# Issuing two of four output stores behind the attention transposes, in a fused attention and MLP kernel

## The chip, the cores and the metric

The kernel runs on one core of a Trainium2 chip. The metric is the device time of one execution in microseconds (us); less is better. Where several executions were timed, the median is given.

## The reference

The first half is sliding-window causal attention for 8 batches, 8 heads, 576 positions and head dimension 64; a query sees itself and the 63 keys before it. The second half is an MLP with a hard-swish over all 4608 rows.

```python
# q, k, v: [8, 8, 576, 64]
scores = (q @ k.T) / sqrt(64)
mask = (rel >= 0) & (rel < 64)            # rel = query position - key position
attn = softmax(where(mask, scores, -1e9)) # over keys
x = (attn @ v).transpose(0, 2, 1, 3).reshape(4608, 512)
h = x @ w_in                              # w_in: [512, 2048]
g = h * clip(h + 3, 0, 6) / 6
out = g @ w_out                           # w_out: [2048, 512], out is float32
```

Matmuls are done in bf16 with sums in f32; inputs and output are f32.

## The kernel before, in words

**Two loops that interleave.** The rows of the MLP are cut into 9 blocks T of 512 tokens. For each block, `s1(T)` (L787) makes h and g: 8 chunks of two 128-wide slices of d_ff, 64 or 128 matmuls (L812), each chunk in one of three PSUM pairs of banks; ACT makes a relu of it (L821), DVE the product (L824) into gT, which frees the pair. Then `s2(T)` (L832) multiplies g with w_out: four output tiles ts = 0 to 3 of 128 rows, 16 matmuls each (L860), so 64 steps n. When a tile is done, `finish` (L870) has ACT copy it from PSUM to an SBUF tile osb (L878), and SP store that tile to the output (256 KB, L883). There are three osb tiles, so the copy of a tile waits for the store of the third tile before it: the copy of ts = 3 waits for the store of ts = 0 of the same block.

**Attention runs inside s2.** During s2(T) TensorE also does the attention of batch b = T + 1, in units put at fixed steps n (`REST`, L925): scores at n = 11 and 18 (L672), products with V at n = 25 (two) and n = 35 (two) (L699). For each of the four groups g of two heads, DVE normalises the product (L737, L740) into a tile opg, and for batches 2 to 7 SP transposes that tile by DMA into xT (L747, in `xdma`); these are called x0 to x3 here. s1(T + 1) reads xT; its first chunk takes the matmuls that need x3 last (L805).

**What else is on the queues.** SP also issues the two DMA transposes of q and k of the batch after that (QKT, L437) once s1(T + 1) is planned to begin, and after these the loads of q (L458, L479) and k (L479) for the batch after that; their f32 data are cast on POOL before they are transposed. ACT issues the loads of v (L384) between its own work.

**Who sets the order.** The order of each engine's queue is written out by a planner, `Plan` (L37), when the kernel is built. Every operation is put into a heap with the time at which it is expected to be ready, a duration, and keys of other operations that must have been placed (`deps`); it is popped in the order of these times, and only then the instruction is emitted. A DMA's duration comes from `moved` (L269). `pl.mark` (L55) notes that a key is done and at what time. An operation whose key isn't marked is parked until it is. So `deps` set the place in a queue; the semaphores that engines wait for on the chip come from the data. In the table of keys, ("x", b, g) is the landing of an x transpose, ("st", nst) that of a store with nst = 4T + ts, ("op", b, g) the normalisation.

The stores of tiles 0 and 1 become ready at about n = 16 and n = 32 of s2, and those of tiles 2 and 3 at n = 48 and 64.

Of the kernel before, what the change touches and what calls it, by code (L numbers as in the profile page):

```python
# [105 lines left out]
def kernel(  # L106
# [11 lines left out]
    B, H, S, D = q.shape  # L118
    DM, FF = moe_w_in.shape
    NT = B * S  # L120
    NG = H // 2
# [3 lines left out]
    SP = KB * P  # L125
# [10 lines left out]
    NR6 = 2  # L136
# [3 lines left out]
    pl = Plan()  # L140
# [21 lines left out]
    def two_banks(readers, dt=F32):  # L162
        i = min(range(len(psums)), key=free_at)
        while free_at(i) >= 1e9:
            pl.pop()
            i = min(range(len(psums)), key=free_at)
        for r in held[i]:
            pl.wait(r)
        held[i] = readers
        return psums[i].tile([P, 2, 512 if dt == F32 else 1024], dt, name=f"ps{i}", tag="ps")  # L170
# [98 lines left out]
    def moved(now, kb, rate):  # L269

        dma["t"] = max(dma["t"], now) + kb / rate
        land = dma["t"] + 1.9 + dma["lag"]
        return max(now + 0.06, dma["t"] - 5.0), land
# [293 lines left out]
    def soft(b, g):  # L567
        return [("mask", b, g)] if b else [("exp", b, g, i) for i in range(2)]

    def vcasts(b, g):  # L570
        return [("cast", b, 2, g // 2, kb) for kb in range(KB)] if b == 0 else [("cast", b, 2, kb) for kb in range(KB)]
# [120 lines left out]
    def pv64(b, g, o):  # L692

        V, W, pT = V_ring[b % 2], W_ring[b % 2], halves.pop((b, g))
        for h in range(2):
            for m in range(KB):
                for odd in range(2):
                    i = min(2 * m + odd, BL - 1)
                    nc.tensor.matmul(  # L699
                        o[odd * D : (odd + 1) * D, h, m * VW : (m + 1) * VW],  # L700
                        lhsT=pT[:, h, i * D : (i + 1) * D],
                        rhs=(V if i % 2 else W)[:, g, m, h, :], start=True, stop=True,
                    )
        pl.pe(0.5)

    def pv128(b, g, o):
        V = V_ring[b % 2]
        pT = P_ring[(b * NG + g) % NPT]
        for h in range(2):
            for qb in range(KB):  # L710
                ob = o[:, h, qb * VW : (qb + 1) * VW]
                nc.tensor.matmul(
                    ob, lhsT=pT[:, h, qb, 0:P], rhs=V[:, g, qb, h, :],
                    start=True, stop=(qb == 0),
                )
                if qb:
                    nc.tensor.matmul(
                        ob, lhsT=pT[:, h, qb - 1, P : 2 * P], rhs=V[:, g, qb - 1, h, :],
                        start=False, stop=True,
                    )  # L720
        pl.pe(0.55)

    def pv(b, g):
        for r in soft(b, g) + vcasts(b, g):
            pl.wait(r)
        o = two_banks([("op", b, g)])
        if b >= NR6:
            pl.need(("w0", b % 2))
            pv64(b, g, o)
        else:  # L730
            pv128(b, g, o)
        pl.mark(("pv", b, g), pl.t)
        ov = o[:, :, 0 : KB * VW].rearrange("p h (k w) -> p h k w", w=VW)
        cell = {}
        def norm(s):
            rec = small.tile([P, 2, KB], F32, name="rec", tag="rec")
            nc.vector.reciprocal(out=rec[:].unsqueeze(3), in_=ov[:, :, :, D:VW])  # L737
            opg = opool.tile([P, KB, 2, D], BF16, name="opg", tag="opg")
            cell["o"] = opg
            nc.vector.tensor_tensor(  # L740
                out=opg[:].rearrange("p k h d -> p h k d"), in0=ov[:, :, :, 0:D],
                in1=rec[:].unsqueeze(3).to_broadcast([P, 2, KB, D]), op=MULT,
            )
        def xdma(t):
            def fn(s):
                x0 = x_at(b)
                nc.sync.dma_start_transpose(  # L747
                    out=xT[:, g, x0 : x0 + SP].rearrange("d (k t) -> d k t", t=P),
                    in_=cell["o"][:].rearrange("p k h d -> p (k h d)"),
                )  # L750
                fr, land = moved(s, 164, 230)
                pl.free["SP"] = fr
                return land
            pl.op("SP", t, 0.1, fn, ("x", b, g))
        m = b * NG + g - 4
        first = (("mask", b, NG - 1),) if b >= NR6 and g == 1 else ()
        pl.op("DVE", pl.t + 0.1, 1.05, norm, ("op", b, g), None if b < NXP else xdma,
              deps=first + ((("x", m // NG, m % NG),) if m >= 0 else ()))
        return cell
# [110 lines left out]
    def finish(T, ts, acc, c0, c1):  # L870
        rows = out[T * TB : (T + 1) * TB]
        rows = rows.rearrange("(p j) d -> j p d", j=J)[ts] if T >= NR6 else rows[ts * P : (ts + 1) * P]
        nst = T * 4 + ts + (c0 > 0)
        cell = {}
        def cp(s):
            osb = osbp.tile([P, DM], F32, name="osb", tag="osb")
            cell["o"] = osb
            nc.scalar.copy(out=osb[:, c0:c1], in_=acc[:, c0:c1])  # L878
            if c0:
                nc.scalar.dma_start(out=rows[:, c0:c1], in_=osb[:, c0:c1])  # L880
        def store(t):
            def fn(s):
                nc.sync.dma_start(out=rows[:, c0:c1], in_=cell["o"][:, c0:c1])  # L883
                fr, land = moved(s, 262, 375)
                pl.free["SP"] = fr
                return land
            pl.op("SP", t, 0.1, fn, ("st", nst))
        pl.op("ACT", pl.t + 0.1, 0.62, cp, ("acc", nst), None if c0 else store,
              deps=(("st", nst - 3),) if nst >= 3 else ())

# [35 lines left out]
    for T in range(NTB):  # L926
# [3 lines left out]
        b = T + 1  # L930
# [36 lines left out]
```

The softmax here doesn't subtract the row's maximum and nothing guards it: scores larger than these inputs give would overflow.

## Time and profile before

| what | value |
|---|---|
| median of 4 runs | 307.53 us (306.58 to 308.46) |
| profiled execution, its time | 308.46 us |
| its span, from first to last instruction | 306.7 us |
| granted TensorE clock, mean | 0.999 |
| busy: TensorE, VectorE, ScalarE, GpSimd | 97%, 54%, 50%, 39% |
| s2's matmuls (L860), busy | 132.7 us |
| s1's matmuls (L812), busy | 126.5 us |
| stores on SP (L883) | 36, median 3.8 us from issue to landing |
| x transposes on SP (L747) | 24, median 3.7 us to landing |
| QKT transposes on SP (L437) | 12, median 8.4 us to landing |

The engines are called PE (TensorE; PEld is its weight load), DVE (VectorE), ACT (ScalarE), POOL (GpSimd) and SP (SyncE, which only issues DMAs). In rows of groups the numbers after the first bar are busy time in us and the mean ns of one instruction, those after the second bar are the idle time of the engine just ahead of the group and what ended most of it. In a timeline a row starts with start and length in us; a number in square brackets is the engine's idle time ahead of it. For a DMA on SPq or ACTq the length is that of the issue, not of the transfer; its landing is the time at which its semaphore says that the data have arrived. In the chain of work, a DMA's piece is the time from issue to landing. In rows of windows, after the limits, come length, then busy us (and number) of PE, PEld, DVE, ACT and POOL, the granted clock, the busy share of the DMA engines and GB/s.

### The profile page before, as it was taken

The numbers are of one execution on the slowest core, as the hardware profiler recorded it, in microseconds if no ns is written. First come the engines' busy times: TensorE is split into PE (matmuls) and PEld (weight loads), VectorE is DVE, ScalarE is ACT, GpSimd is POOL, SyncE is SP. The second block draws the span as 40 slices with busy tenths as digits, with TensorE's granted clock in tenths as the row PEclk, the third lists the DMA queues.
The fourth block names the chain that finished last, engine by engine and source line by source line (L and its number), as shares of the span: only waits on it lengthen the run. The fifth ranks groups of instructions, "written<-read, shape, count | busy, mean of one in ns | idle before, by whom it ended". The sixth has DMA issues, their size and how long they took to land.

```text
span 306.7 us, 6681 instructions
## 1 busy us (share of the span) xinstructions
PE 296.7 (97%) x2787; PEld 153.1 (50%) x2787; DVE 164.1 (54%) x209; ACT 154.8 (50%) x190; POOL 118.9 (39%) x185
## 2 busy tenths in 40 slices
PE   7989989998999999999989999999999999999995
PEld 2554445643544454875434454445665544444443
DVE  5585678656734664466526562667275617304610
ACT  5856686455616661566146713672367236316611
POOL 3167547618834482477027722682252000000000
PEclk9999999999999999999999999999999999999999
DMA  7999999999999999999699979997990550010011
GB/s 218 258 371 387 389 315 252 255 161 286 232 189 238 278 178 156 235 280 190 137 193 280 236 117 225 259 231 121 244 198 11 124 92 0 34 71 34 0 69 71
DMA packets 134863, 58.38 MB, mean 190 GB/s; under 512 B 117296, under 2 KB 124720, under 8 KB 134832
## 3 DMA queue, kind: packets, MB, share of 16 engines
q1 hardware_dynamic: 106560, 50.80, 73.2%
q10 hardware_dynamic: 28272, 7.15, 12.4%
q8 instruction: 22, 0.36, 0.6%
q14 instruction: 9, 0.07, 0.1%
HBM read 36.70 MB, written 9.44 MB: 150 GB/s over the span
## 4 chain that ended last, share of the span: by engine, by line
PE 71%; DMA 14%; SPq 6%; POOL 2%; ACT 2%; issue 2%; DVE 1%; ACTq 0%; POOLq 0%
PE acc L860 33%; PE ps L812 32%; DMA st<-in_moe_w_out_dram 5%; DMA QKT<-nat 3%; DMA st<-in_v_dram 3%; PE ps L699 2%; SPq L357 2%; PE ps L672 2%; DMA xT<-opg 2%; SPq L332 2%; SPq L415 1%; ACT pT L678 1%; POOL wout L280 1%; POOL V L280 1%; DMA tl<-in_k_dram 0%
## 5 line engine op out<-in xcount | busy, mean ns | idle before, releaser
L824 DVE SCALAR_TENSOR_TENSOR gT<-t,ps 128x1024 bf16<-128x1024 bf16 x72 | 87.7, 1220 | 97.3 <-ACT t L821 97.3
L860 PE MATMUL acc<-wout,gT 128*128 128x512 bf16 (+2 forms) x592 | 132.7, 374 | 0.8 <-DVE wout L277 0.5
L812 PE MATMUL ps<-xT,win 128*128 128x512 bf16 (+4 forms) x704 | 126.5, 340 | 2.2 <-DMA xT<-opg 1.3
L821 ACT ACTIVATE t<-ps,half 128x1024 bf16<-128x1024 f32 x72 | 79.9, 1113 | 51.4 <-PE ps L812 50.0
L812 PEld LDWEIGHTS <-win 128*128 128x128 bf16 x704 | 65.2, 98 | 62.1 <-issue 2.9
L860 PEld LDWEIGHTS <-gT 128*128 128x128 bf16 x592 | 54.6, 98 | 61.5 <-issue 1.4
L878 ACT COPY osb<-acc 128x512 f32<-128x512 f32 (+2 forms) x37 | 21.4, 578 | 75.8 <-PE acc L860 72.9
L280 POOL CAST runs<-st 64x512 bf16<-64x512 f32 (+1 forms) x49 | 30.3, 619 | 71.0 <-DMA st<-in_v_dram 55.4
L280 POOL CAST nat<-st 128x512 bf16<-128x512 f32 x48 | 35.2, 758 | 9.8 <-DMA st<-in_k_dram 7.1
L678 ACT ACTIVATE pT<-ps 128x768 bf16<-128x768 f32 x36 | 26.9, 837 | 9.3 <-PE ps L672 9.3
L683 DVE TENSOR_TENSOR pT<-pT,mask 128x1152 bf16<-128x1152 bf16 x24 | 22.2, 944 | 14.9 <-ACT pT L678 14.9
L740 DVE TENSOR_TENSOR opg<-ps,rec 128x640 bf16<-128x640 f32 x32 | 26.4, 824 | 1.1
L280 POOL CAST V<-st 128x512 bf16<-128x512 f32 (+1 forms) x30 | 19.0, 636 | 4.4 <-DMA st<-in_v_dram 2.7
L622 ACT ACTIVATE pT<-ps 128x768 bf16<-128x768 f32 x16 | 12.7, 833 | 0.9 <-PE ps L613 0.8
L277 DVE CAST runs<-st 128x576 bf16<-128x576 f32 x14 | 7.9, 568 | 6.9 <-DMA st<-in_q_dram 5.1
L279 ACT COPY QKT<-ps 128x1152 bf16<-128x1152 bf16 x8 | 9.1, 1135 | 4.2 <-PE ps L582 4.2
L699 PEld LDWEIGHTS <-pT 128*64 128x64 bf16 x480 | 8.6, 111 | 5.1 <-issue 3.0
L280 POOL CAST wout<-st 128x1024 bf16<-128x1024 f32 x6 | 7.4, 1251 | 7.9 <-DMA st<-in_moe_w_out_dram 7.9
L699 PE MATMUL ps<-runs,pT 128*64 128x65 bf16 x288 | 9.9, 196 | 0.0
L672 PEld LDWEIGHTS <-QKT 64*128 64x128 bf16 x432 | 7.3, 95 | 5.1 <-issue 5.1
L699 PE MATMUL ps<-V,pT 128*64 128x65 bf16 x192 | 9.5, 197 | 0.0
L672 PE MATMUL ps<-QKT 64*128 64x64 bf16 x432 | 9.1, 194 | 0.0
(60 smaller groups left out, 119.9 us busy)
## 6 DMA issues: line engine op xcount, KB each, us to landing
out_dram<-osb SPq DMA_DIRECT2D x35, 256.0 KB, 4.1
st<-in_q_dram SPq DMA_DIRECT2D x12, 512.0 KB, 6.8
st<-in_k_dram SPq DMA_DIRECT2D x24, 256.0 KB, 6.3
st<-in_v_dram ACTq DMA_DIRECT2D x24, 256.0 KB, 5.8
st<-in_moe_w_out_dram SPq DMA_DIRECT2D x4, 1024.0 KB, 13.3
st<-in_moe_w_in_dram SPq DMA_DIRECT2D x3, 1024.0 KB, 10.4
st<-in_q_dram SPq DMA_DIRECT2D x8, 288.0 KB, 6.7
st<-in_k_dram SPq DMA_DIRECT2D x8, 288.0 KB, 7.1
```

Source lines behind the costliest of these rows:

```text
L280: return lambda s: nc.gpsimd.tensor_copy(out=out_ap, in_=in_ap) and None
L622: nc.scalar.activation(out=pT[:, :, kbs[0] : kbs[0] + 2, 0:QW], in_=st[:, :, 0 : 2 * QW].rearrange("p h (k w) -> p h k w", k=2), func=EXP, ...
L672: nc.tensor.matmul(st[:, h, c * D : (c + 1) * D], lhsT=kwin(b, g, i, h), rhs=turned(qk(b, 0, g), i)[h * D : (h + 1) * D], start=True, stop ...
L678: nc.scalar.activation(out=pT[:, :, part * NB * D : (part + 1) * NB * D], in_=st[:, :, 0 : NB * D], func=EXP, scale=scale,)
L683: pl.op("DVE", t, 0.8, lambda s: nc.vector.tensor_tensor(out=P_half, in0=P_half, in1=mask64[:].unsqueeze(1).unsqueeze(1).to_broadcast([P, ...
L699: nc.tensor.matmul(o[odd * D : (odd + 1) * D, h, m * VW : (m + 1) * VW], lhsT=pT[:, h, i * D : (i + 1) * D], rhs=(V if i % 2 else W)[:, g, ...
L740: nc.vector.tensor_tensor(out=opg[:].rearrange("p k h d -> p h k d"), in0=ov[:, :, :, 0:D], in1=rec[:].unsqueeze(3).to_broadcast([P, 2, KB ...
L812: nc.tensor.matmul(hs, lhsT=win16[:, g, (2 * c + j) * P : (2 * c + j + 1) * P], rhs=xs, start=(g == 0), stop=(g == NG - 1),)
L821: nc.scalar.activation(out=t1[:], in_=hT[:], func=RELU, bias=half[:], scale=1.0 / 6.0)
L824: nc.vector.scalar_tensor_tensor(out=gT[:, 2 * c : 2 * c + 2, :], in0=cell["t"][:], scalar=1.0, in1=hT[:], op0=MIN, op1=MULT,)
L860: nc.tensor.matmul(accs[ts][:, c0:c1], lhsT=gT[:, fc, ts * P : (ts + 1) * P], rhs=wout16[:, fc, c0:c1], start=(fc == 0), stop=(fc == NFC - 1),
L878: nc.scalar.copy(out=osb[:, c0:c1], in_=acc[:, c0:c1])
```

## The change

The x transposes mark a new key ("xi", b, g) with the time of their issue. In s2(T) with T from 1 to 6, that is beside the attention of batches 2 to 7, the stores of tiles 0 and 1 get the key of x3 as a dependence, so that the planner places them on SP's queue after x3. Before, their places followed from the times at which their copies were done.

```diff
@@ xdma, in pv @@
                     in_=cell["o"][:].rearrange("p k h d -> p (k h d)"),
                 )
+                pl.mark(("xi", b, g), s)
                 fr, land = moved(s, 164, 230)
                 pl.free["SP"] = fr
                 return land
@@ store, in finish @@
                 fr, land = moved(s, 262, 375)
                 pl.free["SP"] = fr
                 return land
-            pl.op("SP", t, 0.1, fn, ("st", nst))
+            held_back = NR6 <= T + 1 < B and ts < 2
+            pl.op("SP", t, 0.1, fn, ("st", nst), deps=(("xi", T + 1, NG - 1),) if held_back else ())
```

NR6 is 2, B is 8 and NG is 4.

## Prediction

> **What bounds the kernel now.** I read the page's busy times first, then its costliest groups, then the stages as windows, the chain of work that ended last, and the timelines of SP, ACT and DVE around the change. The busy times, and the one group of TensorE that waits for anything near the change:
>
> ```profile
> PE 296.7 (97%) x2787; PEld 153.1 (50%) x2787; DVE 164.1 (54%) x209; ACT 154.8 (50%) x190; POOL 118.9 (39%) x185
> L812 PE MATMUL ps<-xT,win 128*128 128x512 bf16 (+4 forms) x704 | 126.5, 340 | 2.2 <-DMA xT<-opg 1.3
> ```
>
> TensorE works for 97% of the span. The column after the second bar is its idle time ahead of the first matmul (s1): 2.2 us in all, 1.3 of them for an x transpose. The row of s2's matmuls (L860) shows 0.8, those of the attention (L672, L699) 0.0. So the change cannot win more than these 2.2 us, and probably only the 1.3.
>
> Where they are is seen in windows from the start of one s1 to that of the next (a window's length follows its limits):
>
> ```profile
> 122.66:153.76 31.10, 31.10 (x345) 20.12 (x344) 17.94 (x20) 15.47 (x18) 15.03 (x23) 1.00 1.00 211
> 153.76:186.32 32.56, 31.28 (x282) 14.93 (x281) 16.55 (x20) 15.48 (x18) 15.00 (x23) 1.00 1.12 207
> 186.32:217.26 30.94, 30.94 (x281) 14.86 (x280) 17.92 (x20) 15.47 (x18) 14.76 (x23) 1.00 1.13 208
> ```
>
> Only the middle one is longer than its PE work, by 32.56 - 31.28 = 1.28 us. The chain names the cause:
>
> ```profile
> 149.91 0.91 SPq L747
> 150.82 0.05 issue
> 150.91 5.55 DMA xT<-opg
> 156.46 0.04 issue
> 156.51 12.68 PE ps L812 x58
> ```
>
> The last x transpose of batch 4, issued at 150.91, lands at 156.46. s1(4) began at 153.76, did the 6 matmuls that don't need it (1.46 us), and stood from 155.22.
>
> SP's queue in s2(2) and in s2(3), where L883 is the store and L747 the x transpose:
>
> ```profile
> 111.11 0.36 SPq L883 DMA_DIRECT2D out_dram<-osb  x1
> 114.57 1.24 SPq L747 DMA_TRANSPOSE xT<-opg  x1
> 115.90 0.53 SPq L883 DMA_DIRECT2D out_dram<-osb  x1
> 116.52 4.66 SPq L747 DMA_TRANSPOSE xT<-opg  x3
> 121.28 0.53 SPq L883 DMA_DIRECT2D out_dram<-osb  x1
> ...
> 142.55 0.57 SPq L883 DMA_DIRECT2D out_dram<-osb  x1
> 146.30 1.24 SPq L747 DMA_TRANSPOSE xT<-opg  x1
> 147.63 0.53 SPq L883 DMA_DIRECT2D out_dram<-osb  x1
> 148.26 3.88 SPq L747 DMA_TRANSPOSE xT<-opg  x3
> 152.23 0.53 SPq L883 DMA_DIRECT2D out_dram<-osb  x1
> ```
>
> Store 0 goes out some 3.5 us ahead of the first x transpose, store 1 between the first and the second, store 2 right behind the fourth.
>
> **Part one: what leaves the path of the x transposes.** Store 0 was issued and had landed (4.1 to 4.6 us) by about the time at which x0 was issued, and x0 waits for its normalisation (DVE ends it at 114.53, the issue is at 114.57). So store 0 is worth nothing here. Store 1 costs its issue, 0.53 us and a gap. But x1 needs its own normalisation: that ends at 116.19 in s2(2) and 147.93 in s2(3), so x1 can move up from 116.52 and 148.26 only by some 0.3 us (0.5 in s2(1)). After that three issues of 1.24 us with gaps of 0.08 run on SP, and the normalisations are ahead of them. Besides, in s2(2), s2(4) and s2(5) one of the three issues took 1.98, 1.71 and 1.71 us in place of 1.24, and x1 landed 4.4, 4.3 and 5.1 us after its issue; in the other three stages 2.9, 2.6 and 2.7. In those same stages store 1 landed late (4.3 to 4.5 us, against 2.8 in s2(3) and s2(6)). I read this as a queue filled by store 1, so x3 wins another 0.5 to 0.7 us there: about 0.3 us earlier in s2(3) and s2(6), 0.5 in s2(1), 0.8 to 1.0 in the others.
>
> What is that worth? x3 lands at +1.1, +0.7, +2.7, +0.5, +1.1 and 0.0 us from the start of the s1 that reads it (s2(1) to s2(6)), and is needed at about +1.4. Only the third is late. An issue 0.3 us earlier takes 0.3 of its 1.28 us for sure; the rest depends on the landing, which took 5.5 us there and 3.4 to 4.8 in the other five. Store 1 was no part of that, for it had landed at 150.4, before x3 was issued. With a landing of the others' kind, x3 comes at 150.6 + 3.9 = 154.5, and all 1.28 us are gone. I take that: the 5.5 is the one outlier. The ends are a gain of 0.3 and of 1.28; a loss here is possible only if the stores now close behind x3 slow it, and store 2 stood there before.
>
> **Part two: what is put behind x3.** Two stores of 0.53 us and gaps, 1.2 us of SP, stand ahead of store 2 and the two QKT transposes. With x3 earlier by 0.3 to 1.0, these are issued 0.2 to 0.9 us later, and with 512 KB more in the queue ahead of them. At store 2's 3.5 to 4.7 us to landing I allow 2 us more in all. QKT has cover: in s2(3) the second one is issued at 157.56 and lands 8.6 us later, at 166.2; the scores that read it begin at 171.56. That is 5.4 us, and 4.9 to 5.5 around the other stages. The k loads that wait for QKT end at 142.45 in s2(3), 3.8 us ahead of x0 (146.30), and at 173.7 in s2(4), 4.1 us ahead. The casts on POOL for the next QKT end at 146.3 in s2(3), against an issue at 152.87. All this costs nothing while the delay stays below 3.8 us; every microsecond beyond would be one of x0, and then of x3.
>
> **Part three: the new wait.** There are three output tiles (osb), so the fourth copy of a stage (ACT, L878) waits until store 0 has landed. That was long so; now store 0 is issued just behind x3. In ACT's queue the relus of the next s1 stand behind that copy, behind them the DVE products and the PSUM banks that TensorE's fourth chunk needs. From ACT and DVE around the start of s1(3), at 122.66:
>
> ```profile
> 122.91 0.58 ACT L878 COPY osb<-acc 128x512 f32<-128x512 f32 x1 [2.91 <-PE acc L860]
> 124.61 1.11 ACT L821 ACTIVATE t<-ps,half 128x1024 bf16<-128x1024 f32 x1 [1.12 <-PE ps L812]
> 125.75 1.22 DVE L824 SCALAR_TENSOR_TENSOR gT<-t,ps 128x1024 bf16<-128x1024 bf16 x1 [7.51 <-ACT t L821]
> ```
>
> The copy can begin as late as 124.0 without moving the relu (ACT has 1.12 us of idle time there). DVE frees the first bank pair at 125.75 + 1.22 = 126.97, and TensorE comes to its fourth chunk at 122.66 + 3 x 13.97/8 = 127.90: another 0.93 us. So the wait is hidden while store 0 lands before s1's start + 2.3 us. Beyond that each microsecond is one of TensorE, in each of six stages.
>
> Nearest row for store 0: store 2 of today, issued at the same place right behind x3. It lands 3.8, 3.5, 4.7, 3.7, 3.8 and 3.7 us after its issue in s2(1) to s2(6). Store 0's issue, by the times of part one, is at about 88.9, 120.2, 151.95, 183.4, 215.1 and 245.35. That makes landings at +0.9, +1.0, +2.9, +0.8, +1.7 and +0.7 from the next s1. Five are hidden; the one in s2(3) costs 0.6 us if the bad landing recurs, nothing with the others' 3.8. The ends: with the 5.5 us of the slowest x transpose everywhere, the overrun is 0.3 + 0.75 + 1.4 + 0.3 + 1.0 + 0.2 = 3.95 us; with the slowest of all stores (7.3 us) 1.8 us more per stage, 14.8 in all. Less than nothing is excluded, since the wait is new.
>
> Against the change speaks a rule of the Trainium skill (DMA: Bandwidth & Descriptors, on HWDGE ordering): a DMA's completion increment is written only after every earlier write of the same DMA engine, on whatever queue. By it store 0 waits also for the first v load, which ACT issues 0.4 to 1.3 us ahead of x3's end and which lands at 92.7, 122.8, 154.0, 186.3 and 218.1, that is +0.9, +0.1, +0.2, 0.0 and +0.8: before my landings. The second v load starts with the very copy that waits (122.93), so it can't precede store 0. Rule and row give the same sum; I keep the row, because store 2 has already paid for all of this.
>
> **The sum.** The profiled execution took 308.46 us, 306.7 of it span and 1.76 around it. Less 1.28, plus 0 to 0.6, that is 307.2 to 307.8. The median of the four runs, 307.53, is 0.93 below this execution, so a typical run seems to lose less to such a late landing than the one shown: the gain from the median is perhaps 0.4, and I forecast 307.1. The fastest run, 306.58, is roughly what a run without the wait takes.
>
> **Rivals.**
> (a) Nothing happens: x3's landing is set by what lies around it, store 0 is hidden. 307.5. For it: 5.5 us had nothing to do with store 1.
> (b) The fourth copy becomes the bound. Three stores, then QKT, next to v loads that take 5.3 to 7.4 us to land at this place: store 0 lands 5.5 us after issue, beyond the +2.3 at which it decides, 3.95 us are added and the 1.28 won: 307.53 + 2.7 to 3.95 = 310.2 to 311.5, taken as 310.6. Against it: store 2's own landings.
> (c) More is won than one wait: x3 up to 1 us earlier spares other runs all their late landings, 307.53 - 2.2 = 305.3 at most; taken as 305.8.
> (d) The order doesn't come out as meant, since a planner writes the queues: its copy may take another place on ACT. By the planner's costs store 0 lands at about 17.1 us of s2 and the copy is due at 17.55, so I expect ACT's order as it is; otherwise the copy falls behind the first relu, which costs nothing: 307.5.
>
> **Chances.** Forecast 0.43 (306.3 to 308.0 as its own range), (a) and (d) together 0.25, (b) 0.27, (c) 0.05. A measurement here can tell 0.5%, 1.54 us, from no change: below 305.99 is faster, 0.05; above 309.07 slower, 0.25, since a small overrun of (b) stays within; within 0.70. The range reaches from 306.1 to 310.4: it leaves out (c) and the upper half of (b).
>
> **What would show it.** Right: SP shows four x transposes in a row, the last three within 3.9 us, then three stores; the wait of L812 for xT falls from 1.3 to below 0.3; the fourth copy starts up to 1.3 us later in a stage while the relu behind it moves by less than 0.6. Wrong: L878 waits for out_dram, and L812 for the DVE product (gT) in several stages, or L672 waits for QKT.

## The result and the profile after

The changed kernel takes 308.6 us (median of 43 runs) against 307.7 us for the kernel before (64 runs in the same comparison): ratio 1.0028, 95% interval 1.0014 to 1.0042. That is about 0.9 us more, inside the stated range, but the other way than the forecast of 307.1 us. The same kernel was measured twice more beside the experiments, with 1.0065 (1.0040 to 1.0091) and 1.0038 (1.0014 to 1.0062).

The execution that was profiled with the result was disturbed (1716.76 us, the matmuls of s1 and s2 over four times their length), so the lines below are from the run "after_second" of the same kernel: 307.7 us, of which 306.0 are span. Its code is one to two lines longer, so L813 is the L812 of before, L861 is L860, L822 is L821, L879 is L878 and L884 is L883.

The busy times and the groups that answer to those shown of before, with ACT's relu and copy added (after the second bar: idle time ahead of the group, and what ended it):

```profile
PE 297.1 (97%) x2787; PEld 153.1 (50%) x2787; DVE 163.4 (53%) x209; ACT 154.0 (50%) x190; POOL 120.1 (39%) x185
L813 PE MATMUL ps<-xT,win 128*128 128x512 bf16 (+4 forms) x704 | 127.0, 340 | 1.0 <-DVE gT L825 0.7 <-DMA xT<-opg 0.3
L822 ACT ACTIVATE t<-ps,half 128x1024 bf16<-128x1024 f32 x72 | 79.5, 1114 | 41.1 <-PE ps L813 34.9 <-POOL runs L280 3.2 <-DVE gT L825 2.9
L879 ACT COPY osb<-acc 128x512 f32<-128x512 f32 (+2 forms) x37 | 21.4, 579 | 86.1 <-PE acc L861 58.2 <-DMA out_dram<-osb 23.3 <-PE ps L813 4.6
```

ACT's same two groups in before:

```profile
L821 ACT ACTIVATE t<-ps,half 128x1024 bf16<-128x1024 f32 x72 | 79.9, 1113 | 51.4 <-PE ps L812 50.0 <-DVE gT L824 1.3
L878 ACT COPY osb<-acc 128x512 f32<-128x512 f32 (+2 forms) x37 | 21.4, 578 | 75.8 <-PE acc L860 72.9 <-DMA st<-in_v_dram 2.9
```

TensorE's idle time for x is shorter (0.3 us instead of 1.3), as meant. In its place it now waits for gT, the product that frees a PSUM pair, and ahead of that ACT stands: its copies wait 23.3 us for stores (about 2.9 us ahead of each of these copies it stood idle before too, for TensorE), and its relus show 3.2 us "for POOL", of which nothing was seen before. SP around s2(4) and s1(5):

```profile
175.83 7.00 SPq L747 DMA_TRANSPOSE xT<-opg  x4
182.92 1.49 SPq L884 DMA_DIRECT2D out_dram<-osb  x3
184.51 9.34 SPq L437 DMA_TRANSPOSE QKT<-nat  x2
193.94 0.53 SPq L884 DMA_DIRECT2D out_dram<-osb  x1
```

Four x transposes in a row, then three stores, then QKT: the order is what the change says. No other queue's order changed.

The five s1 that follow a changed s2 and have attention around them are compared best by their own length, from the first L813 to the first L861. Undisturbed they take 13.81 us (13.97 where x comes in two pieces, s1(3) and s1(6)). Three of them, s1(2), s1(4) and s1(5), of after_second:

```profile
90.53:104.67 14.14, 13.97 (x65) 6.25 (x64) 7.71 (x7) 8.31 (x8) 7.01 (x12) 1.00 1.19 271
...
153.06:166.89 13.83, 13.83 (x66) 6.24 (x65) 7.62 (x7) 8.19 (x8) 5.98 (x10) 1.00 1.27 224
184.02:198.82 14.80, 14.12 (x65) 6.25 (x64) 7.79 (x7) 8.07 (x8) 7.00 (x12) 1.00 1.21 244
```

The excess of the five is 0.33 + 0.17 + 0.02 + 0.99 + 0.39 = 1.90 us. In the trace of before it was 1.54, 1.45 of it in s1(4), for the one late x transpose. The place of the loss has changed: s1(4) is clean, s1(5) lost a microsecond.

What each piece waited for is seen when the starts of the matmuls are laid beside those of an undisturbed s1 of the same kind in before: where the distance grows by a step, TensorE lost time, and the matmul there has a releaser. The largest step of after_second, in s1(5):

```profile
197.10 1.89 PE L813 MATMUL ps<-xT,win 128*128 128x512 bf16 x8 [0.68 <-DVE gT L825]
```

This is the eighth and last chunk, and the step is 0.84 us. (It is more than the idle time shown, because the ends of matmuls are modelled.) Of the 1.90 us, 0.81 are steps for xT (s1(2) 0.33, s1(5) 0.16, s1(6) 0.32), so the x transposes are not always in time now either. Steps for gT at the eighth chunk make 1.01 (s1(3) 0.17, s1(5) 0.84), and one at the fourth chunk, in s1(6), 0.07. In after_again, the other trace of the changed kernel, the excess is 1.21: 1.16 for gT at the eighth chunk (0.28, 0.22 and 0.66 in s1(2), s1(3) and s1(5)), 0.05 at the fourth, none for x.

The traces with the old order (before, before_osb4, before_oneq, before_osb4_oneq, before_tailsp below) have 1.54, 0.50, 0.50, 0.26 and 1.87 us, and those with one store held 0.30 and 1.63, all of it for x. These sums scatter too much, from one execution to the next, to stand for the 0.9 us that was measured. But TensorE waits for gT in these five s1 only where both stores are held.

### The profile page after: what moved, and what is told of

It reads as the page before. It is cut to its first block, busy times and chain, and to the rows that moved or that the text cites. A ratio compares the mean times of both kernels' runs of the same rounds, so it can differ in the third digit from the quotient of the medians.

```text
span 1715.0 us, 6681 instructions
## 1 busy us (share of the span) xinstructions
PE 1710.8 (100%) x2787; PEld 541.8 (32%) x2787; DVE 159.0 (9%) x209; ACT 160.5 (9%) x190; POOL 107.9 (6%) x185
## 4 chain that ended last, share of the span: by engine, by line
PE 100%; DVE 0%; ACT 0%; issue 0%; ACTq 0%
PE acc L861 45%; PE ps L813 44%; PE ps L699 2%; PE ps L672 2%; PE ps L582 1%; PE ps L613 1%; PE ps L607 1%; PE ps L898 1%; PE ps L712 1%; PE ps L766 1%; PE ps L717 1%; DVE idle L204 0%; ACT osb L879 0%; ACTq L879 0%
## 5 line engine op out<-in xcount | busy, mean ns | idle before, releaser
L861 PE MATMUL acc<-wout,gT 128*128 128x512 bf16 (+2 forms) x592 | 770.7, 1658 | 0.0
L813 PE MATMUL ps<-xT,win 128*128 128x512 bf16 (+4 forms) x704 | 764.8, 1470 | 0.0
L813 PEld LDWEIGHTS <-win 128*128 128x128 bf16 x704 | 229.6, 329 | 532.8 <-issue 530.8
L861 PEld LDWEIGHTS <-gT 128*128 128x128 bf16 x592 | 173.1, 300 | 503.8 <-issue 502.8
L822 ACT ACTIVATE t<-ps,half 128x1024 bf16<-128x1024 f32 x72 | 80.1, 1113 | 685.8 <-PE ps L813 685.8
L879 ACT COPY osb<-acc 128x512 f32<-128x512 f32 (+2 forms) x37 | 21.2, 574 | 622.6 <-PE acc L861 622.6
L699 PEld LDWEIGHTS <-pT 128*64 128x64 bf16 x480 | 38.2, 338 | 31.7 <-issue 31.7
L699 PE MATMUL ps<-runs,pT 128*64 128x65 bf16 x288 | 41.6, 422 | 0.0
L699 PE MATMUL ps<-V,pT 128*64 128x65 bf16 x192 | 40.0, 472 | 0.0
L672 PE MATMUL ps<-QKT 64*128 64x64 bf16 x432 | 36.4, 440 | 0.0
L712 PE MATMUL ps<-V,pT 128*128 128x65 bf16 x80 | 25.0, 465 | 0.0
L582 PE MATMUL ps<-ident,runs 64*64 64x64 bf16 x288 | 24.4, 431 | 0.0
```

The source lines that it names most:

```text
L582: nc.tensor.transpose(out=tr[h, i, j * NP : (j + 1) * NP], in_=runs[i][b * NG + g][h, j, :], identity=ident[h, h],)
L672: nc.tensor.matmul(st[:, h, c * D : (c + 1) * D], lhsT=kwin(b, g, i, h), rhs=turned(qk(b, 0, g), i)[h * D : (h + 1) * D], start=True, stop ...
L699: nc.tensor.matmul(o[odd * D : (odd + 1) * D, h, m * VW : (m + 1) * VW], lhsT=pT[:, h, i * D : (i + 1) * D], rhs=(V if i % 2 else W)[:, g, ...
L712: nc.tensor.matmul(ob, lhsT=pT[:, h, qb, 0:P], rhs=V[:, g, qb, h, :], start=True, stop=(qb == 0),)
L813: nc.tensor.matmul(hs, lhsT=win16[:, g, (2 * c + j) * P : (2 * c + j + 1) * P], rhs=xs, start=(g == 0), stop=(g == NG - 1),)
L822: nc.scalar.activation(out=t1[:], in_=hT[:], func=RELU, bias=half[:], scale=1.0 / 6.0)
```

## Where the time went

ACT's queue around s1(5) in after_second (ACTq rows are the issue of v loads):

```profile
186.22 0.59 ACT L879 COPY osb<-acc 128x512 f32<-128x512 f32 x1 [4.87 <-DMA out_dram<-osb]
...
191.60 1.11 ACT L822 ACTIVATE t<-ps,half 128x1024 bf16<-128x1024 f32 x1 [0.93 <-PE ps L813]
193.94 0.63 ACTq L384 DMA_DIRECT2D tl<-in_v_dram  x1
194.68 3.12 ACT L822 ACTIVATE t<-ps,half 128x1024 bf16<-128x1024 f32 x3 [1.97 <-POOL runs L280]
```

and at the same place in before:

```profile
193.26 1.11 ACT L821 ACTIVATE t<-ps,half 128x1024 bf16<-128x1024 f32 x1 [0.61 <-PE ps L812]
193.34 1.17 ACTq L384 DMA_DIRECT2D tl<-in_v_dram  x1
194.99 1.11 ACT L821 ACTIVATE t<-ps,half 128x1024 bf16<-128x1024 f32 x1 [0.61 <-PE ps L812]
```

In before, the last v load (tl, 64 rows) is issued right after the start of a relu, 7.2 us from s1's start at 186.16. In after_second it is issued 9.9 us from s1's start (184.02), ACT stands 1.97 us, and the three relus behind it run without a gap, for their matmuls were done meanwhile. What was ACT waiting for? The first QKT transpose of that stage, in the same trace, has this landing:

```profile
L437 SPq DMA_TRANSPOSE QKT<-nat x1: 4097/4097/4097, 184.5 to 184.5; - x1
...
DMA to landing us min/median/max: 9.4/9.4/9.4
```

184.51 + 9.4 = 193.9: the v load goes out when QKT lands. The instruction with which ACT waits for semaphores ahead of that load stands in the trace too:

```profile
L384 ACTq EVENT_SEMAPHORE  x1: 2282/2282/2282, 191.6 to 191.6; - x1
```

It takes 2.28 us, from 191.62 to 193.90, and one of its two semaphores is the one that QKT's landing raises. In s1(2) to s1(4) QKT lands at 98.8, 131.0 and 161.5, and the load is issued at 98.89, 131.05 and 161.52. SP's long issue of the second QKT transpose isn't what holds it: that ended at 99.84, 131.19 and 161.83, after the load had gone out. The relu's "POOL" in the profile is only the releaser that came last by time.

No data pass from QKT to that load. So not all the semaphores that engines wait for come from the data, as the account of the planner had it. The link is in the built program: every DMA of SP and ACT takes one of eight completion semaphores in turn, in the order in which the planner emits them, and a DMA first waits until the one that had its semaphore before has landed. That is the eighth DMA back. (In the trace, the 191 DMAs of the two engines use eight semaphores, 23 or 24 times each.) Numbered in that order, a stage of the changed kernel reads:

```
 94 SP  store 0        95 SP  store 1        96 ACT v load 0     97 SP  store 2
 98 SP  QKT 0 (q)      99 SP  QKT 1 (k)     100 ACT v load 1    101 SP  store 3
102 SP  q load 0      103 ACT v load 2      104 SP  q load 1    105 ACT v load 3 (waits for  97)
106 ACT v tail (waits for 98 = QKT 0)       107 SP  q tail (waits for 99)
```

The kernel before has the same link: its v tail also waits for its QKT 0. But there QKT 0 landed 5.8, 6.5, 7.9 and 6.7 us after s1's start (s1(2) to s1(5)), and ACT comes to the load at about 7.2, or 8.6 in s1(4), which stood for x. ACT came 0.4 to 1.4 us after the landing. In after_second QKT 0 lands at 8.3, 9.2, 8.4 and 9.9 us. It is issued later behind two stores, and with three stores ahead of it takes 8.3 to 9.4 us to land instead of 7.0 to 8.8.

How long may ACT stand there? The same waiting instruction took 0.86 to 1.45 us in seven stages of after_second, after_again, after_osb4 and hold_store1 (the last two are below), and TensorE lost nothing at the eighth chunk. In six stages it took 1.94 to 2.57 us, and TensorE lost 0.17 to 0.84. So in these traces the PSUM pairs hid waits of up to 1.45 us.

## The experiments

Theories, as they stood in the expectations: A, the fourth copy waits for the held store 0 (rival (b) of the prediction); B, QKT and the k loads come too late for the attention; C, three stores behind x3 slow its landing; D, the held stores push QKT, and the last v load holds ACT until it has landed. Ratios are to the kernel before on the same chip.

**The changed kernel again (after_again).** No edit.

> The changed kernel as it is, for a trace of it. Theory A (the fourth copy waits for the held store 0, and the relus behind it reach TensorE): ratio to before 1.001 to 1.005; ACT's copies show 3 to 8 us of waits for the output stores, and s1's matmuls wait for the product gT, 1 to 3 us over the six stages. Theory B (QKT and the k loads come too late behind the stores): s1 waits 0, but the attention's scores or the x transposes of the next batch are late, x0 issued over 1 us later within its stage. Theory C (three stores close behind x3 slow its landing): s1's wait for xT grows from 1.3 us to 2 or more, x3 lands over 4.5 us after its issue in most stages.

Measured 1.0065 (1.0040 to 1.0091). The copies waited 21.3 us for stores, far more than A's 3 to 8, yet TensorE waited only 0.5 us for gT. The ratio is above A's range too. x3 landed 3.3 to 4.2 us after its issue, so C fell. B's signs (late scores or x0) were absent. But its v tail was issued at 101.08, 132.41, 162.47 and 194.99 with QKT landing at 101.0, 132.4, 162.4 and 194.9: this trace is where theory D came from.

**A fourth output tile (after_osb4).** The second mask reuses an f32 tile of the first to make room.

```diff
-    osbp = ctx.enter_context(tc.tile_pool(name="osb", bufs=3))
+    osbp = ctx.enter_context(tc.tile_pool(name="osb", bufs=4))
-    mask32 = consts.tile([P, QW], F32, name="mask32")
+    mask32 = neg32
-              deps=(("st", nst - 3),) if nst >= 3 else ())
+              deps=(("st", nst - 4),) if nst >= 4 else ())
```

> The changed kernel with a fourth osb tile, so that the fourth copy of a stage waits for a store of the stage before and no longer for store 0; the order on SP stays. Room is made by letting the second mask reuse the first one's f32 tile at the start. Theory A: the loss is gone, ratio 0.996 to 1.000. Theories B and C: unchanged, 1.002 to 1.004.

Measured 1.0004 (0.9985 to 1.0023). The copies' waits for stores are gone. TensorE still lost 0.80 us in s1(5), where ACT stood 2.24 us at the v tail, issued at 193.29 while QKT landed at 193.2. The point is at A's upper end. After_again, on the same chip, has 1.0040 to 1.0091, which lies above this interval, so the fourth tile does win something back. The traces don't show where all of it comes from: at the fourth chunk, where A's wait would reach TensorE, only 0.05 and 0.07 us were lost in the two traces of the changed kernel. The wait that is left isn't A's.

**One store held at a time (hold_store1, hold_store0).**

```diff
-            held_back = NR6 <= T + 1 < B and ts < 2
+            held_back = NR6 <= T + 1 < B and ts == 1     # hold_store1;  ts == 0 for hold_store0
```

> Only the second store of each stage is held behind x3, the first goes out ahead of x0 as before. Theory A: store 0 has landed long before the fourth copy, so no loss, 0.996 to 1.000, with x3 as early as in the full change. Theories B and C: about half of the loss, 1.001 to 1.002.

Measured 0.9993 (0.9967 to 1.0020).

> Only the first store of each stage is held behind x3, the second stays between x0 and x1. Theory A: the whole loss, since the fourth copy waits as in the full change and x3 is as late as before: 1.002 to 1.006. Theories B and C: about half of the loss, 1.001 to 1.002.

Measured 1.0010 (0.9983 to 1.0037). The intervals don't part the theories, and A's expectation for hold_store0 rested on a mistake: the tile that the fourth copy gets is the one whose store comes first in the order of issue, and that is now store 1. By the built program's waits and the trace this copy doesn't wait for store 0 (it begins at 152.93 in s1(4), store 0 lands at 155.4). So in both runs A's wait is gone and only half of the push on QKT is left. In hold_store0 QKT 0 lands 8.2, 7.8, 8.4 and 7.2 us after s1's start, ACT's waits at the v tail are 0.8 and 0.95 us in two stages, none in the others, and the five s1 have 0.30 us of excess together. In hold_store1 these waits are 1.0 and 1.2 us in two stages; its excess, 1.63 us, is all for late x transposes.

**One q load of 1 MB (after_oneq and before_oneq).** This takes one DMA out between QKT 0 and the v tail, so that the tail's semaphore is that of store 2.

```diff
-                for hh in range(2):
+                for hh in range(1):
...
-                            out=T["t"][:, 4 * hh : 4 * hh + 4, :],
-                            in_=src[b, 4 * hh : 4 * hh + 4, 0 : J * P, :].rearrange(...)
+                            out=T["t"][:],
+                            in_=src[b, :, 0 : J * P, :].rearrange(...)
...
-                        for g in (2 * hh, 2 * hh + 1):
+                        for g in range(NG):
```

> The changed kernel with each batch's two q loads of 512 KB (batches 2 to 7) made one of 1 MB. There are eight DMA semaphores, taken in turn in the order of issue, and a DMA waits for the landing of the eighth one before it. In the changed kernel the last v load of a stage (tl, on ACT, ahead of a relu) is the eighth after the first QKT transpose; with one DMA less between them it waits for store 2, which is early. Theory D (the held stores push QKT, and the last v load holds ACT until QKT has landed): ACT's semaphore waits of 2 us at L384 are gone, the ratio falls by 0.002 to 0.004 against the changed kernel, to 0.999 to 1.002, and what is left is the fourth copy's wait (theory A, 1 to 2 us behind s1's start, as before). Theory A alone: ratio as in the changed kernel, 1.003 to 1.006.

> The kernel before with the same single q load, as the control. All theories: 0.997 to 1.003, since the last v load found its semaphore free anyway; it shows what the single load does by itself.

Measured 0.9981 (0.9962 to 0.9999) for the change with it and 1.0010 (0.9988 to 1.0032) for the kernel before with it. That is a little below D's range for the first and within the range of the second. The single load by itself does nothing that can be seen; under it the change turns from a loss into a small gain. The trace of after_oneq, again around s1(5), which begins at 184.38:

```profile
191.65 1.11 ACT L822 ACTIVATE t<-ps,half 128x1024 bf16<-128x1024 f32 x1 [0.61 <-PE ps L813]
191.73 0.82 ACTq L384 DMA_DIRECT2D tl<-in_v_dram  x1
193.38 1.11 ACT L822 ACTIVATE t<-ps,half 128x1024 bf16<-128x1024 f32 x1 [0.61 <-PE ps L813]
```

The tail is issued 7.35 us after s1's start, though QKT 0, issued at 184.8, lands 9.2 us later, at 194.0. QKT is as late as in the change, and nobody minds. What is left of the excess is 0.65 us. Of it 0.46 are in s1(4), at the fourth chunk and for gT: the fourth copy began only after store 0 had landed at 155.6, 2.6 us into that s1. The rest is for x.

**Both (after_osb4_oneq) and its controls (before_osb4, before_osb4_oneq).** The edits are the two above together.

> The changed kernel with the fourth osb tile and the single q load. Theories A and D together: neither the fourth copy nor the last v load holds ACT, so only the gain of earlier x transposes is left: 0.995 to 0.999, TensorE idle ahead of s1's matmuls under 0.3 us in the six stages, and better than either alone. Theory C (x3 slowed by the stores behind it): no better than 1.000.

> The kernel before with a fourth osb tile, the control for the same step in the changed kernel. All theories: 0.998 to 1.002, for the copies find a free tile anyway.

> The kernel before with the fourth osb tile and the single q load, the control for the best version so far. If the order of the stores is what makes that version faster: 0.998 to 1.003. If the tile and the load do it by themselves: 0.995 to 0.998.

Measured 0.9975 (0.9952 to 0.9998), and for the controls 0.9997 (0.9967 to 1.0026) and 0.9997 (0.9968 to 1.0026). The excess of the five s1 is 0.08 us, the least of all traces. It is the fastest version, 306.66 us median, but after_oneq lies within its interval: what the fourth tile adds isn't settled, and neither is its lead over before_osb4_oneq.

**The suspected wait made larger (after_tailsp) and its control (before_tailsp).** The v tail goes out from SP. That moves it ahead of the q loads, and v load 3 becomes the eighth DMA after QKT 0, on ACT and a chunk earlier.

```diff
-                nc.scalar.dma_start(
+                (nc.sync if kb == KB - 1 else nc.scalar).dma_start(
...
-                    pl.op("ACT", s + (VGAP2 if b == NR6 else VGAP), 0.45, issue(kb + 1))
+                    pl.op("SP" if kb + 1 == KB - 1 else "ACT", s + (VGAP2 if b == NR6 else VGAP), 0.1 if kb + 1 == KB - 1 else 0.45, issue(kb + 1))
```

> The changed kernel with the last v load of a stage issued from SP, which also moves it ahead of the q loads in the order of issue; so the fourth v load, still on ACT and a chunk earlier than the last, is now the eighth DMA after the first QKT transpose. Theory D: ACT now waits about 3.5 us for QKT instead of 2, one chunk earlier, and the loss grows: 1.008 to 1.025. Theory A alone: as the changed kernel or a little better, 1.002 to 1.005.

> The kernel before with the last v load issued from SP, the control for the run that lost 2%. Here too the fourth v load on ACT is the eighth DMA after the first QKT transpose, but QKT has no held stores ahead of it and landed 5.7 to 7.9 us after s1's start in the trace of before, against about 5.4 at which this load is due. Theory D: ACT waits 0.3 to 2.5 us in each stage, partly hidden, ratio 1.000 to 1.010, so that at least half of the 2% is due to the held stores. If the shift of the load were itself the cause, with no part of QKT's place: 1.018 or more.

Measured 1.0212 (1.0176 to 1.0249) with the held stores, and 0.9985 (0.9963 to 1.0008) without, the latter just below D's 1.000 to 1.010. From the waits of after_tailsp (in total, times, longest):

```profile
ACT t L822 <- DMA QKT<-nat: 7.1, 2, 3.6
PE ps L813 <- DVE gT L825: 5.3, 4, 2.0
```

and ACT in s1(5) of that trace:

```profile
194.20 1.11 ACT L822 ACTIVATE t<-ps,half 128x1024 bf16<-128x1024 f32 x1 [0.61 <-PE ps L813]
198.46 0.39 ACTq L384 DMA_DIRECT2D st<-in_v_dram  x1
198.94 2.12 ACT L822 ACTIVATE t<-ps,half 128x1024 bf16<-128x1024 f32 x2 [3.63 <-DMA QKT<-nat]
```

Here the profile itself names QKT: issued at 189.1, landed at 198.4, and the load follows at 198.46. The s1 takes 18.01 us in place of 13.81. Of these 4.2 us, 2.2 are a step for gT and 0.3 for x. The other 1.7 were lost while the granted clock was 0.50, from 202.3 to 205.7, where matmuls came every 0.43 us instead of 0.22. That began 0.9 us after the end of the wait; the stages s1(3) and s1(4), with steps of 1.93 and 1.85 us for gT, have no such stretch. In the control QKT 0 lands at 192.5 and the load goes out at 192.55, some 1.3 us late, which the PSUM pairs hide: that s1 takes 13.81.

**The changed kernel with these controls (after_second).** No edit.

> The changed kernel once more, on the same chip as these controls and for a second trace. Theory D with A: ratio 1.001 to 1.006; ACT's last v load begins, to within 0.1 us, when the first QKT transpose lands in most of s1(2) to s1(5), 0.5 to 2.3 us later than ACT is ready for it; TensorE's idle time ahead of s1's matmuls is for the product gT and not for xT.

Measured 1.0038 (1.0014 to 1.0062), as D expects; its trace is the one shown above. ACT's wait ahead of the v tail took 0.88, 1.94, 1.30 and 2.28 us in the four stages. That TensorE would wait for gT and not for xT was half right: 1.07 us against 0.81.

## Why the prediction was wrong, step by step

**The bound and the place of the gain** were right: the wait for x was the only one to win. Its size was that of one bad execution. In before it cost 1.5 us; the other traces with the old order lost 0.26 to 0.50 us for x, and 1.86 in one. With both stores held, and the v tail on ACT, it was 0.81, 0, 0.24, 0.20 and 0.07.

**Part one, x3 earlier**, was half right. Against s1's start x3 is issued earlier by 0.3 to 1.1 us in four stages of after_second. In s2(4) and s2(5) it is later, by 0.8 and 0.4: from x1's issue to x2's it again took 2.3 and 2.1 us there in place of 1.3, with no store between them. That store 1 had filled the queue was a wrong reading of the long issues; what makes them long is open. Two smaller readings were off. In before, store 0 landed 0.8 to 1.1 us after x0's issue in four stages, and 3.4 us after it in s2(1). And s1(2), s1(5), s1(6) and s1(7) begin some 0.16 us before the times that were used (186.16, not 186.32).

**Part two, "All this costs nothing while the delay stays below 3.8 us", is the step that failed.** Against s1, QKT 0 lands 0.5 to 3.2 us later in s1(2) to s1(5), where 2 us had been allowed for, and 4.0 in s1(6). The named covers held: no scores waited for QKT. But I followed QKT's landing to those who use its data, the scores (5.4 us of cover) and the k loads (3.8), and not to those who use its semaphore. ACT comes to the v tail 0.4 to 1.4 us after QKT's landing in before. Relus stand behind that load, then the DVE products, then TensorE, which lost time when ACT's wait was 1.94 us or more. In before the tail was issued within 0.9 us of QKT's landing in three of four stages; the rows were there (landing 129.1 and issue 129.93, 192.8 and 193.34), and I had read only the first v load.

**Part three, the copy behind store 0**, named a true wait with a price near the truth. Store 0 landed at +1.9, +1.9, +2.2, +2.1, +2.6 and +0.7 us, about 1 us later than forecast in four stages, since it was issued up to 1.7 us later than forecast there, or, in s1(2), took 4.4 us to land. The point of decision at +2.3 held. In after_oneq, where of the two waits of ACT only this one is left, s1(4) at +2.6 lost 0.46 us, near the 0.6 that was forecast for a landing at +2.9. The one stage beyond it in after_second, s1(6) at +2.6, lost only 0.07 us by it, because TensorE was already 0.32 us late there for the third x transpose, x2.

**The rule of the Trainium skill** on the order of completion (DMA: Bandwidth & Descriptors, Queues, rings and completion order), weighed there, didn't decide anything: store 0 landed 0.5 to 2.0 us after the first v load in the five stages that have one.

**The sum** had -1.28 and +0 to 0.6. The missing term is ACT's stand at the v tail. It took up to 2.28 us of ACT and 0.84 of TensorE in the worst stage, and 1.01 and 1.16 us of TensorE in the two traces of the changed kernel. Without it the change is a small gain (0.9981, and the single load alone has 1.0010), with it 1.0028. Rival (b) had the sign and the engine, but another instruction. By the steps of TensorE the tail took nearly all of what ACT cost, and the copy 0.05 to 0.07 us. By the ratios the division isn't settled: removing either wait brought the change to about 1.000 or below.

## What to carry to other kernels

A DMA that is moved takes with it every wait on its landing, and not all of these come from data: where completion semaphores are handed out in turn, the DMA that takes its semaphore next (here the eighth after it) waits too, on whatever engine issues that one. So list what the built program makes each DMA wait for before pushing a slow transfer back, and look above all for a DMA issue on a compute engine, because the work queued behind it there stops. A releaser in a profile that has no reason to release (POOL ahead of a relu) is a hint to compare the time with the landings.

## What the runs showed that was not expected

The more stores of 256 KB are issued between x3 and the QKT transpose, the longer QKT takes to land. From issue to landing, the mean of QKT 0 in s1(2) to s1(6) is 6.7 to 7.6 us in the five traces with one store there, 7.9 and 8.2 in the two with two, and 8.9 to 9.3 in the six with three.

Where the second v load of a stage waits behind a late copy, the fourth needs longer to issue: in s1(2), s1(3) and s1(5) of after_second it took 1.14 to 1.94 us, against 0.37 to 0.38 in before. With the fourth output tile, where the copy isn't late, it took 0.37 in four of five stages. The three loads go out closer together then; whether that is the cause isn't shown.
